# dK and dV of a sliding-window attention block made transposed on four column groups of TensorE, and W_up's late transposes issued earlier

## The chip, the cores and the metric

The kernel runs on one core of a Trainium2 chip. The metric is the device time of one execution in microseconds; a time is the median over several executions. A core has TensorE (PE in the profile, with its weight loads as PEld), VectorE (DVE), ScalarE (ACT), GpSimd (POOL) and SyncE (SP), each with its own instructions in order, and 16 DMA engines fed by queues that the engines issue to.

## What is computed

The kernel computes the output and all gradients of a gated mix of two branches: attention with a sliding window (32 heads of 16, window 256) and a feed-forward block with a ReLU gate. Cut to what matters:

```python
def _A_ref(x, wqkv, wo):
    B, S, D = x.shape                          # 1, 2048, 512
    H = 32; Dh = D // H; W = 256
    q, k, v = ...                              # (x @ wqkv), split into heads
    scores = jnp.einsum("bhqd,bhkd->bhqk", q, k) * (Dh ** -0.5)
    mask = (idx[:, None] - idx[None, :] >= 0) & (idx[:, None] - idx[None, :] < W)
    p = _softmax(jnp.where(mask[None, None], scores, -1e9), axis=-1)
    o = jnp.einsum("bhqk,bhkd->bhqd", p, v)
    return ... @ wo
def _B_ref(x, W_gate, W_up, W_down):           # F = 1376
    gate = x @ W_gate; up = x @ W_up
    return (gate * (gate > 0) * up) @ W_down

g = sigmoid((x * gate_w).sum(-1, keepdims=True))
out = g * _A_ref(x, A_wqkv, A_wo) + (1 - g) * _B_ref(x, B_W_gate, B_W_up, B_W_down)
# outputs: out and the gradients of x, wqkv, wo, W_gate, W_up, W_down, gate_w for a given grad_out
```

## The kernel before

Positions are cut into 16 tiles of 128 (NT), the 512 features into 4 column blocks (DC), each of which holds 8 heads (HG). There are three stages.

The first stage is the feed-forward block with its gradients in one loop over 11 blocks of F and 4 groups of 512 positions.

The second stage is the attention loop. Its order is written out by hand: an engine gets its instructions in the order in which the Python code emits them. The loop runs over turns (184 of them hold products). A turn takes two pairs of heads and up to two blocks of scores, each a query tile qb by a key tile kb, and emits in this order:

- `products`: on PE, the scores S of this turn and D = dO V^T of the turn before. Heads have 16 features, so these matmuls use 16 or 32 of the array's rows, and four row groups can work side by side.
- `front`: the exponential on ACT, from S in PSUM into PP in SBUF; `mask` on POOL; `gradp` on DVE, which multiplies PP by D.
- for some units, the transposed probabilities (`flip`): either a DMA transpose on SP's queue (line 779), or eight transposes on PE (line 787) into a PSUM tile `pt` and a copy out of it. The turned blocks lie in tiles P2, 14 buffers in all.
- `some_sums`: matmuls of `rowsum` (lines 746 and 748) with PP as weights, which collect row sums, the output and parts of dQ for a query tile in BA. When a query tile is complete ("closed"), BA is copied to BAs, and `small_ops` on DVE and POOL make from it `rq`, which holds, for each head, three groups of 16 columns: the first two are multiplied by P, the third by dS.
- `cd_piece`: two or more pieces a turn, three turns or more after the closing. A piece is four heads of one pair (kb, qb): for each head two matmuls (lines 497 and 500) with a turned block of P2 as 128 x 128 weights and 32 or 16 columns of rq streamed. They sum dK and dV of key tile kb in CD (one buffer), keys on the partitions. After a key tile's last piece, one copy brings CD to `rows_st`.
- PE flips, then `background` work: the next projections (`pp`), the transposes of K and V (`ptp`) and the gradient of wqkv of the column block before (`wps`).

The tiles `pt`, `ptp`, `pp` and `wps` share a tag "tr" of two PSUM buffers. CD and BA have one buffer each. `share` puts a copy on ACT or DVE, whichever has less work by a running estimate of costs (`busy`).

A list `plan` gives, by group of the projections, weight loads and DMA transposes of weights for the third stage; they wait in `late` and one of them is issued every second or fourth turn. The slots x0 to x3, d0 to d3 and p0 to p3, which hold inputs in transposed form at first, are used again for them.

The third stage goes over the 16 position tiles: `bps` (feed-forward output), `aps` (attention output), `dxps` (gradient of x, with W_gate, W_up and wqkv in turned form) and `wo_ps`. Its loads come by groups of two tiles (`load_group`). Between the second and the third stage stands a seam: the loads of group 0 (line 843 to 885), then the transposes of W_up for its blocks 4 to 10 (line 528), then `clear("Wu")`, which sets the rest of the last block to zero on POOL (line 531). In tile 0, the W_up part of dxps comes last.

Of the kernel before, what the change touches and what calls it, by code (L numbers as in the profile page):

```python
# [22 lines left out]
def kernel(  # L23
# [21 lines left out]
    P = 128  # L45
# [31 lines left out]

    busy = {"act": 0.0, "dve": 0.0}

    def share(out, in_, n, half=False, by=None, sbuf=False):  # L80
        cost = {"act": 0.11 + n * (0.00098 if sbuf else 0.00078),
                "dve": 0.08 + n * (0.00036 if sbuf else 0.00051 if half else 0.001)}
        eng = min(("act", "dve"), key=lambda e: busy[e] + cost[e])
        busy[eng] += cost[eng]
        if by is None:
            evac(out, in_, eng)
        elif eng == "act":
            nc.scalar.mul(out, in_, by)
        else:
            nc.vector.tensor_scalar(out, in_, by, None, op0=ALU.mult)  # L90
# [381 lines left out]
    if True:  # L472
# [8 lines left out]
        P2 = {}  # L481
        RQ = {}
        CDs = {}
        BAt = {}
        BAsb = {}
        sts = {}

        def cd_piece(c, kb, qb, half, last):
            if (c, kb) not in CDs:
                CDs[(c, kb)] = [psr.tile([P, HG, 2 * Dh], F32, tag="CD", bufs=1, name="CD"), True]  # L490
            cd = CDs[(c, kb)]
            rq = RQ[(c, qb)]
            for g in (2 * half, 2 * half + 1):
                p2 = P2[(c, qb, kb, g)]
                for pr in range(2):
                    h = 2 * g + pr
                    nc.tensor.matmul(cd[0][:, h, :], lhsT=p2[:, 0, pr, :], rhs=rq[:, h, 0:2 * Dh],  # L497
                                     start=cd[1], stop=True, skip_group_check=True)
                    cd[1] = False
                    nc.tensor.matmul(cd[0][:, h, 0:Dh], lhsT=p2[:, 1, pr, :], rhs=rq[:, h, 2 * Dh:3 * Dh],  # L500
                                     start=False, stop=True, skip_group_check=True)
            if last:
                share(sts[c][:, kb, 1:3, :].rearrange("p a (h d) -> p h a d", h=HG),
                      cd[0][:].rearrange("p h (a d) -> p h a d", a=2), 2 * P)
                if kb % 4 == 3 and (kb < NT // 2 or c == DC - 1):
                    spill(c, kb - 3)

        def spill(c, t0):
            tsl = slice(t0, t0 + NT // 4)
# [46 lines left out]
        def load_wo():  # L556
            for k0 in range(0, DC, 2):
# [6 lines left out]
                11: turns("wqkv", A_wqkv, 8, 12, "p2"),  # L564
                12: turns("Wg", B_W_gate, 0, 4, "x0") + turns("Wg", B_W_gate, 4, 8, "d0"),
                13: turns("Wg", B_W_gate, 8, 12, "x1") + turns("Wu", B_W_up, 0, 4, "d1") + [lambda: clear("Wg")],
                15: loads("Wd", B_W_down, 0, "x3") + loads("Wd", B_W_down, 4, "d3") + loads("Wd", B_W_down, 8, "p3") + [load_wo]}

        def grad_parts(c, seam=False):
            hold = {}  # L570
# [167 lines left out]
        def rowsum(u, i, qb, first, last):  # L738
            kb = u.blocks[i][1]
            kv = proj[(u.c, kb // TPG)]["kv"]  # L740
            if first:
                BAt[(u.c, qb)] = psr.tile([P, HG, 50], F32, tag="BA", bufs=1, name="BA")
            BA = BAt[(u.c, qb)]
            for pr in range(2):
                h = 2 * u.g + pr
                nc.tensor.matmul(BA[:, h, 0:33], lhsT=u.PP[:, 0, 2 * i + pr, :], rhs=kv[:, kb % TPG, h, 1:34],  # L746
                                 start=(first and pr == 0), stop=True, skip_group_check=True)
                nc.tensor.matmul(BA[:, h, 33:50], lhsT=u.PP[:, 1, 2 * i + pr, :], rhs=kv[:, kb % TPG, h, 0:17],  # L748
                                 start=False, stop=True, skip_group_check=True)
            if last:  # L750
                BAs = wk.tile([P, HG, 50], F32, tag="BAs", name="BAs")
                share(BAs[:], BA[:], HG * 50)
                BAsb[(u.c, qb)] = BAs

        def place(u):
            if u.edge:
                if u.at not in wides:
                    wides[u.at] = wide("p2")
                p2 = wides[u.at][:, u.x if u.nb == 2 else 0, :, :, :]
            elif u.at < 2 and u.x == 0:  # L760
                if "p2" not in wides:
                    wides["p2"] = wide("p2")
                p2 = wides["p2"][:, u.at, :, :, :]
            elif u.nb == 2 or u.x == 0:
                p2 = pools["p2"].tile([P, 2, 4, P], BF, tag="P2", bufs=14, name="p2")[:]
                wides[u.at] = p2
            else:
                p2 = wides[u.at]
            for i, (qb, kb) in enumerate(u.blocks):
                b = 2 * (i if u.nb == 2 else u.x)  # L770
                P2[(u.c, qb, kb, u.g)] = p2[:, :, b:b + 2, :]
            return p2
# [89 lines left out]
        def load_group(g):  # L862
# [15 lines left out]
                load_f(dgT_g, dgT_d, gsl)  # L878
            duT_g = S2["g6"].tile([P, FC, GT * P], BF, tag="duT_g")
            load_f(duT_g, duT_d, gsl)  # L880
            o_g = S2["g6"].tile([P, GT, DC, P], BF, tag="o_g", name="o_g")
            for t in range(GT):
                t0 = (g * GT + t) * P
                nc.sync.dma_start(o_g[:, t, :, :], dqkvo_d[t0:t0 + P, :].rearrange("p (c a n) -> p c a n", c=DC, a=4)[:, :, 3, :])
            nc.sync.dma_start(go_g[:] if g == 0 else go_g, go_d[gsl, :].rearrange("(t p) d -> p t d", p=P))
            return hT_g, dgT_g, duT_g, T_g, go_g, o_g

        with tc.manual_schedule():
# [47 lines left out]
                        break  # L936
                return total

            while turn < NI + 3 or ev or cdq or bg or sums:
                for e in busy:  # L940
                    busy[e] = max(0.0, busy[e] - 2.3) + (1.0 if e == "act" else 1.25)
                now = ev.pop(turn, [])
# [40 lines left out]
                if turn == 0:  # L983
                    behind.pop(0)()
                    behind.pop(0)()
                    background()
                    background()
                elif behind:
                    behind.pop(0)()
                if turn == 2:  # L990
                    fend.close()
                    pools["p2"] = p3b.enter_context(tc.tile_pool(name="attp2", bufs=2, side="right"))
# [2 lines left out]
                        flip(v)  # L995
                fresh = not sums or not sums[0][3] or (sums[0][0].c, sums[0][2]) == (0, 0) or turn > max(closed.values())
                some_sums(fresh)
                due = turn - 3 - closed.get(cdq[0][0:1] + cdq[0][2:3], turn) if cdq else 0
                for _ in range(4 if not us else 3 if due >= 3 else 2):
                    if cdq and closed.get(cdq[0][0:1] + cdq[0][2:3], turn) + 3 <= turn:  # L1000
                        piece = cdq.pop(0)
                        cd_piece(*piece)
                        if piece[4]:
                            break
                copies = []
                for w in flips.get(turn, []):
                    if not w.dma:
# [41 lines left out]
            S2["g6"] = ctx.enter_context(tc.tile_pool(name="g6", bufs=2))  # L1049
            S2["t6"] = ctx.enter_context(tc.tile_pool(name="t6", bufs=2))  # L1050
            grp_next = load_group(0)
            for f in turns("Wu", B_W_up, 4, 8, "x2") + turns("Wu", B_W_up, 8, 12, "d2"):
                f()
            clear("Wu")
            for f in S2["grads"]:
                store = f()
                if store is not None:
# [4 lines left out]
    with ExitStack() as p56:  # L1062
        x_r5 = x_r

        with ExitStack() as p6:
# [18 lines left out]
            for g in range(NG):  # L1084
# [3 lines left out]
                for tl in range(GT):  # L1088
# [27 lines left out]
                    amb = t6.tile([P, D], F32, tag="amb")  # L1116
                    nc.vector.tensor_tensor(out=amb[:], in0=a_sb[:], in1=bps[:], op=ALU.subtract)
                    nc.gpsimd.tensor_tensor(out=amb[:], in0=amb[:], in1=go_g[:, tl, :], op=ALU.mult)
                    dz = t6.tile([P, 4], F32, tag="dz")
                    nc.vector.reduce_sum(dz[:, 0:1], amb[:], axis=AX.X)  # L1120
                    nc.vector.tensor_tensor(out=dz[:, 1:2], in0=g_all[:, t:t + 1], in1=omg_all[:, t:t + 1],
# [89 lines left out]
```

## Time and profile before

| | us |
|---|---|
| median of 3 runs | 880.09 (880.01 to 880.79) |
| the profiled execution | 881.28 |
| its span from first to last instruction | 879.6 |
| PE busy in the span | 856.6 |
| DVE, POOL, ACT busy | 507.9, 478.5, 393.5 |
| mean granted clock of TensorE | 0.998 |

In the profile, a group of instructions has its line, engine, operation, the tiles written and read (buffer numbers left out), and its shapes; "128\*128 128x32" is a matmul with weights of 128 rows and 128 columns and a stream of 32. After the bar stand the busy time in us and the mean in ns of one, and after a second bar the engine's idle time just before the group with what ended it. Matmuls overlap in the array, so their durations add up to more than the time they take; the distance between starts tells their pitch. In a timeline the rows have start, duration, engine, line, operation, tiles and shapes, and neighbours of one kind are merged ("x8"). "SPq" is SP's issue of DMAs.

### The profile page before, as it was taken

Reading aid. Unit: us, or ns where it says so; the run is one execution under the profiler, and the core shown is the slowest. Engines: PE = TensorE matmul, PEld = TensorE weight load, DVE = VectorE, ACT = ScalarE, POOL = GpSimd, SP = SyncE. Lnnn points to the kernel's source line nnn. Section 1 sums busy time; section 2 is a strip of 40 time slices with the busy share of each in tenths; the row PEclk is TensorE's granted clock in tenths of the full one; section 3 lists DMA queues with packets and bytes.
Section 4 is the critical chain, followed back from the end, with each engine's and each line's share of the span. In section 5 each row is a group of like instructions: output and inputs, shape, how many; then the busy total and the mean of one; then the engine's idle time right before and its main releaser. Section 6 shows DMA issues by size and latency. Waiting matters only on the chain. (4 is left out here: it accounts for less than half of the span.)

```text
span 879.6 us, 29392 instructions
## 1 busy us (share of the span) xinstructions
PE 856.6 (97%) x12563; PEld 557.2 (63%) x12563; DVE 507.9 (58%) x764; ACT 393.5 (45%) x567; POOL 478.5 (54%) x887
## 2 busy tenths in 40 slices
PE   8999999999999999999999999999999899999998
PEld 5566655665567877767777777777777444444444
DVE  4445543333278888877888788887785132222223
ACT  5522222223366576756667666576654111111111
POOL 2644444444357777876778667786776222222111
PEclk9999999999999999999999999999999999999999
DMA  9999999999877999789998989999999999777731
GB/s 289 220 190 201 210 204 211 207 206 199 193 126 122 150 156 158 115 132 160 178 142 109 144 166 187 153 136 162 182 203 208 227 284 210 182 177 189 180 90 49
DMA packets 443132, 154.08 MB, mean 175 GB/s; under 512 B 371608, under 2 KB 440568, under 8 KB 443000
## 3 DMA queue, kind: packets, MB, share of 16 engines
q1 hardware_dynamic: 439400, 146.03, 88.7%
q0 software_dynamic: 2016, 5.64, 1.8%
q8 instruction: 98, 1.61, 0.8%
q10 hardware_dynamic: 1584, 0.53, 0.3%
q14 instruction: 34, 0.28, 0.1%
HBM read 32.15 MB, written 36.24 MB: 78 GB/s over the span
## 5 line engine op out<-in xcount | busy, mean ns | idle before, releaser
L729 DVE TENSOR_TENSOR PP<-PP,D 128x1024 bf16<-128x1024 bf16 (+1 forms) x184 | 219.0, 1190 | 53.8 <-POOL PP L722 17.5
L712 ACT ACTIVATE PP<-S 128x1024 bf16<-128x1024 f32 (+1 forms) x184 | 185.2, 1006 | 96.7 <-PE D L679 51.2
L722 POOL TENSOR_SCALAR_AFFINE_SELECT PP<-PP 128x512 bf16<-128x512 bf16 (+1 forms) x188 | 143.3, 763 | 77.7 <-ACT PP L712 75.3
L74 DVE COPY p<-pt 128x1024 bf16<-128x1024 bf16 x163 | 111.6, 685 | 10.6 <-PE pt L787 10.6
L356 POOL TENSOR_TENSOR hgu<-rg,upm 128x512 bf16<-128x512 bf16 x44 | 50.8, 1154 | 119.9 <-DVE upm L354 103.5
L787 PE MATMUL pt<-ident,PP 128*128 128x128 bf16 x1496 | 113.0, 218 | 0.1
L746 PE MATMUL BA<-KV,PP 128*128 128x33 bf16 x1440 | 106.6, 180 | 2.1 <-ACT BAs L72 1.6
L746 PEld LDWEIGHTS <-PP 128*128 128x128 bf16 x1440 | 85.7, 96 | 31.3 <-issue 11.7
L748 PE MATMUL BA<-KV,PP 128*128 128x17 bf16 x1440 | 102.4, 170 | 0.0
L396 PE MATMUL wps<-hgu_r,x_r 128*128 128x256 bf16 x640 | 96.0, 273 | 0.0
L497 PE MATMUL CD<-rq,p 128*128 128x32 bf16 x1440 | 94.8, 176 | 0.0
L500 PE MATMUL CD<-rq,p 128*128 128x16 bf16 x1440 | 93.6, 169 | 0.0
L748 PEld LDWEIGHTS <-PP 128*128 128x128 bf16 x1440 | 84.6, 96 | 10.9 <-issue 7.5
L787 PEld LDWEIGHTS <-PP 128*128 128x128 bf16 x1496 | 85.2, 97 | 0.2 <-issue 0.2
L497 PEld LDWEIGHTS <-p 128*128 128x128 bf16 x1440 | 80.7, 95 | 0.3
L500 PEld LDWEIGHTS <-p 128*128 128x128 bf16 x1440 | 80.5, 96 | 0.3
L396 PEld LDWEIGHTS <-x_r 128*128 128x128 bf16 x640 | 62.6, 98 | 28.3
L679 PE MATMUL S<-zT,K 32*128 32x128 bf16 (+3 forms) x1056 | 77.5, 238 | 0.4 <-ACT PP L712 0.2
L679 PE MATMUL D<-zT,V 32*128 32x128 bf16 (+3 forms) x1056 | 72.2, 237 | 4.9 <-DVE PP L729 4.3
L354 DVE SCALAR_TENSOR_TENSOR upm<-rg,ups 128x512 bf16<-128x512 bf16 x44 | 30.2, 687 | 80.3 <-PE ups L341 55.5
L1107 ACT COPY a_sb<-aps 128x512 f32<-128x512 f32 x16 | 9.3, 584 | 136.9 <-issue 107.3
L364 POOL TENSOR_TENSOR hgu<-dh_sb,rg 128x512 bf16<-128x512 bf16 x44 | 58.7, 1334 | 9.0 <-ACT dh_sb L362 9.0
(155 smaller groups left out, 1519.7 us busy)
## 6 DMA issues: line engine op xcount, KB each, us to landing
hgu_d<-hgu SPq DMA_DIRECT2D x44, 384.0 KB, 3.5
dqkvo_d<-rows_st SPq DMA_DIRECT2D x14, 512.0 KB, 4.5
duT_g<-hgu_d SPq DMA_DIRECT2D x8, 640.0 KB, 5.8
gt<-hgu_d SPq DMA_DIRECT2D x7, 640.0 KB, 5.9
dgT_g<-hgu_d SPq DMA_DIRECT2D x7, 640.0 KB, 4.9
p<-PP SPq DMA_TRANSPOSE x173, 4.0
out_dram<-wst SPq DMA_DIRECT2D x20, 128.0 KB, 3.0
go_in<-in_grad_out_dram SPq DMA_DIRECT2D x4, 512.0 KB, 8.7
```

The costliest lines, as they stand in the source:

```text
L74: nc.vector.tensor_copy(out, in_)
L364: nc.gpsimd.tensor_tensor(out=k.hgu[:, 2, :], in0=dh_sb[:], in1=k.rg[:], op=ALU.mult)
L396: nc.tensor.matmul(acc["w"][:, c, :], lhsT=x_r[:, t, c * P:(c + 1) * P], rhs=k.dgu_r[:, :, i, :], start=(go_ and c % 2 == 0), stop=no_, sk ...
L497: nc.tensor.matmul(cd[0][:, h, :], lhsT=p2[:, 0, pr, :], rhs=rq[:, h, 0:2 * Dh], start=cd[1], stop=True, skip_group_check=True)
L500: nc.tensor.matmul(cd[0][:, h, 0:Dh], lhsT=p2[:, 1, pr, :], rhs=rq[:, h, 2 * Dh:3 * Dh], start=False, stop=True, skip_group_check=True)
L679: nc.tensor.matmul(dst, lhsT=proj[(u.c, kb // TPG)][nm + ("", "1")[par]][rows[par], (kb % TPG) * P:(kb % TPG + 1) * P], rhs=proj[(u.c, qb ...
L712: nc.scalar.activation(two[:].rearrange("p x a b q -> p x a (b q)")[:, :, 0, 0:n], flat(us[0].S[:], n), ACT.Exp)
L722: nc.gpsimd.affine_select(out=out, in_=out, compare_op=ALU.is_ge, fill=0.0, base=0 if up else -1, pattern=[[0, 2], [0, b1 - b0], [1 if up ...
L729: nc.vector.tensor_tensor(out=v(1), in0=v(0), in1=flat(vs[0].D[:], n), op=ALU.mult)
L746: nc.tensor.matmul(BA[:, h, 0:33], lhsT=u.PP[:, 0, 2 * i + pr, :], rhs=kv[:, kb % TPG, h, 1:34], start=(first and pr == 0), stop=True, ski ...
L748: nc.tensor.matmul(BA[:, h, 33:50], lhsT=u.PP[:, 1, 2 * i + pr, :], rhs=kv[:, kb % TPG, h, 0:17], start=False, stop=True, skip_group_check ...
L787: nc.tensor.transpose(pt[:, a, b if u.nb == 2 else 2 * u.x + b, :], u.PP[:, a, b, :], ident[:])
```

## The change

In `cd_piece` the operands change places. The weights are now 32 or 16 columns of rq, and a turned block of P2 (128 columns) is streamed. The four heads of a piece write to four groups of 32 partitions of CD, so dK and dV are collected transposed, features on the partitions. `cd_piece` comes right behind the products in a turn, ahead of the sums. After a key tile's last piece, ACT copies CD to `cdT` in bf16; one turn later `cd_rows` (called from the list `backs`, ahead of the flips) turns it back by two transposes on PE into a "tr" buffer, `ptc`, and ACT copies that to `rows_st`. `share` gets an argument that names the engine; the copies of CD, ptc and BA name ACT. P2 has 13 buffers.

Of W_up's transposes, those of blocks 4 to 7 go into `plan`, behind the loads of W_down, and those of blocks 8 to 10 into `load_group(0)`, ahead of the loads of o and behind that of grad_out, which is itself ahead of the o loads now in each group. `clear("Wu")` is issued in tile 0 of the third stage, behind the product `amb` on POOL.

```diff
-    def share(out, in_, n, half=False, by=None, sbuf=False):
+    def share(out, in_, n, half=False, by=None, sbuf=False, eng=None):
...
-        eng = min(("act", "dve"), key=lambda e: busy[e] + cost[e])
+        eng = eng or min(("act", "dve"), key=lambda e: busy[e] + cost[e])
...
         def cd_piece(c, kb, qb, half, last):
             if (c, kb) not in CDs:
-                CDs[(c, kb)] = [psr.tile([P, HG, 2 * Dh], F32, tag="CD", bufs=1, name="CD"), True]
-            cd = CDs[(c, kb)]
+                CDs[(c, kb)] = psr.tile([P, 2, 2, P], F32, tag="CD", bufs=1, name="CD")
+            cd = CDs[(c, kb)][:, 0, :, :]
             rq = RQ[(c, qb)]
-            for g in (2 * half, 2 * half + 1):
-                p2 = P2[(c, qb, kb, g)]
-                for pr in range(2):
-                    h = 2 * g + pr
-                    nc.tensor.matmul(cd[0][:, h, :], lhsT=p2[:, 0, pr, :], rhs=rq[:, h, 0:2 * Dh],
-                                     start=cd[1], stop=True, skip_group_check=True)
-                    cd[1] = False
-                    nc.tensor.matmul(cd[0][:, h, 0:Dh], lhsT=p2[:, 1, pr, :], rhs=rq[:, h, 2 * Dh:3 * Dh],
-                                     start=False, stop=True, skip_group_check=True)
+            for a, d0, d1 in ((0, 0, 2 * Dh), (1, 2 * Dh, 3 * Dh)):
+                for h in range(4 * half, 4 * half + 4):
+                    r0 = 32 * (h % 4)
+                    nc.tensor.matmul(cd[r0:r0 + d1 - d0, half, :], lhsT=rq[:, h, d0:d1], rhs=P2[(c, qb, kb, h // 2)][:, a, h % 2, :],
+                                     start=(qb == kb and half == 0 and a == 0), stop=True, skip_group_check=True)
             if last:
-                share(sts[c][:, kb, 1:3, :].rearrange("p a (h d) -> p h a d", h=HG),
-                      cd[0][:].rearrange("p h (a d) -> p h a d", a=2), 2 * P)
-                if kb % 4 == 3 and (kb < NT // 2 or c == DC - 1):
-                    spill(c, kb - 3)
+                cdT = wk.tile([P, 2, P], BF, tag="cdT", name="cdT")
+                share(cdT[:], cd, 2 * P, eng="act")
+                backs.append((turn + 1, lambda: cd_rows(c, kb, cdT)))
+
+        def cd_rows(c, kb, cdT):
+            pt = ps.tile([P, 2, P], BF, tag="tr", bufs=2, name="ptc")[:]
+            for k in range(2):
+                nc.tensor.transpose(pt[:, k, :], cdT[:, k, :], ident[:])
+            share(sts[c][:, kb, 1:3, :].rearrange("p a (h d) -> p h a d", h=HG),
+                  pt.rearrange("p s (h a d) -> p (s h) a d", h=4, a=2), 2 * P, True, eng="act")
+            if kb % 4 == 3 and (kb < NT // 2 or c == DC - 1):
+                spill(c, kb - 3)
...
-                15: loads("Wd", B_W_down, 0, "x3") + loads("Wd", B_W_down, 4, "d3") + loads("Wd", B_W_down, 8, "p3") + [load_wo]}
+                15: loads("Wd", B_W_down, 0, "x3") + loads("Wd", B_W_down, 4, "d3") + loads("Wd", B_W_down, 8, "p3") + turns("Wu", B_W_up, 4, 8, "x2") + [load_wo]}
...
-                share(BAs[:], BA[:], HG * 50)
+                share(BAs[:], BA[:], HG * 50, eng="act")
...
-                p2 = pools["p2"].tile([P, 2, 4, P], BF, tag="P2", bufs=14, name="p2")[:]
+                p2 = pools["p2"].tile([P, 2, 4, P], BF, tag="P2", bufs=13, name="p2")[:]
...
             load_f(duT_g, duT_d, gsl)
+            nc.sync.dma_start(go_g[:] if g == 0 else go_g, go_d[gsl, :].rearrange("(t p) d -> p t d", p=P))
+            if g == 0:
+                for f in turns("Wu", B_W_up, 8, 12, "d2"):
+                    f()
             o_g = S2["g6"].tile([P, GT, DC, P], BF, tag="o_g", name="o_g")
...
-            nc.sync.dma_start(go_g[:] if g == 0 else go_g, go_d[gsl, :].rearrange("(t p) d -> p t d", p=P))
...
                 elif behind:
                     behind.pop(0)()
+                due = turn - 3 - closed.get(cdq[0][0:1] + cdq[0][2:3], turn) if cdq else 0
+                for _ in range(4 if not us else 3 if due >= 3 else 2):
+                    if cdq and closed.get(cdq[0][0:1] + cdq[0][2:3], turn) + 3 <= turn:
+                        piece = cdq.pop(0)
+                        cd_piece(*piece)
+                        if piece[4]:
+                            break
...
                 some_sums(fresh)
-                due = turn - 3 - closed.get(cdq[0][0:1] + cdq[0][2:3], turn) if cdq else 0
-                for _ in range(4 if not us else 3 if due >= 3 else 2):
-                    if cdq and closed.get(cdq[0][0:1] + cdq[0][2:3], turn) + 3 <= turn:
-                        piece = cdq.pop(0)
-                        cd_piece(*piece)
-                        if piece[4]:
-                            break
+                while backs and backs[0][0] <= turn:
+                    backs.pop(0)[1]()
...
             grp_next = load_group(0)
-            for f in turns("Wu", B_W_up, 4, 8, "x2") + turns("Wu", B_W_up, 8, 12, "d2"):
-                f()
-            clear("Wu")
...
                     nc.gpsimd.tensor_tensor(out=amb[:], in0=amb[:], in1=go_g[:, tl, :], op=ALU.mult)
+                    if t == 0:
+                        clear("Wu")
```

More of the change, by code (lines that the diff above doesn't have):

```diff
@@ L483 @@
         CDs = {}
+        backs = []
         BAt = {}
@@ L937, in some_sums @@
                 return total
-            while turn < NI + 3 or ev or cdq or bg or sums:
+            while turn < NI + 3 or ev or cdq or bg or sums or backs:
                 for e in busy:
```

## The prediction

> **What bounds the kernel now.** I read the page first, then the busy time by stretch, then the list of waits, then the timeline of some turns of the attention loop, and last the end of that loop.
>
> ```profile
> span 879.6 us, 29392 instructions
> ...
> PE 856.6 (97%) x12563; PEld 557.2 (63%) x12563; DVE 507.9 (58%) x764; ACT 393.5 (45%) x567; POOL 478.5 (54%) x887
> ```
> ```profile
> 400.00:500.00 100.00, 97.37 (x2305) 73.38 (x2303) 82.91 (x119) 66.23 (x92) 76.51 (x172) 1.00 0.99 143
> ...
> 670.00:710.00 40.00, 36.75 (x349) 20.68 (x346) 8.78 (x21) 7.52 (x15) 15.79 (x31) 0.96 1.07 246
> ```
> ```profile
> PE D L679 <- DVE PP L729: 4.3, 11, 0.6
> ```
>
> The columns of the stretches are length, then busy time (and instructions) of PE, PEld, DVE, ACT and POOL, the granted clock and the DMA share. The exponentials, one for each turn of the attention loop, span 240 to 668 us:
>
> ```profile
> L712 ACT ACTIVATE PP<-S x184: 592/1023/1044, 240.0 to 668.1; 128x1024 bf16<-128x1024 f32 x176, 128x512 bf16<-128x512 f32 x8
> ```
>
> In the middle of the loop PE is busy 97 of 100 us, while DVE has 17 us free and ACT 34. Among the waits (us in total, times, longest), PE's largest on another engine is 4.3 us in all. So PE's own order sets the time of the loop: what is taken from it shortens the loop, what is added or made to wait on it lengthens it. DMA is nearly full too (0.99), but no large wait of PE is for a turned tile of probabilities. A busy PE says nothing of its pitch, so the costs below are start-to-start distances in the timeline (start, duration, engine, line, operation, tiles, shapes, count).
>
> ```profile
> 453.52 0.28 PE L679 MATMUL S<-zT,K 16*128 16x256 bf16 x2
> 453.53 0.29 PE L679 MATMUL D<-zT,V 16*128 16x128 bf16 x4
> 453.64 0.27 PE L679 MATMUL S<-zT,K 32*128 32x256 bf16 x2
> 453.85 0.19 PE L746 MATMUL BA<-KV,PP 128*128 128x33 bf16 x1
> ...
> 454.27 0.18 PE L497 MATMUL CD<-rq,p 128*128 128x32 bf16 x1
> 454.29 0.17 PE L500 MATMUL CD<-rq,p 128*128 128x16 bf16 x1
> ...
> 454.85 0.17 PE L500 MATMUL CD<-rq,p 128*128 128x16 bf16 x1
> 454.87 0.61 PE L787 MATMUL pt<-ident,PP 128*128 128x128 bf16 x8
> 455.32 0.59 PE L149 MATMUL pp<-x,p 128*128 128x512 bf16 x2
> 455.84 0.28 PE L679 MATMUL S<-zT,K 16*128 16x256 bf16 x2
> 455.85 0.28 PE L679 MATMUL D<-zT,V 16*128 16x256 bf16 x2
> 455.96 0.27 PE L679 MATMUL S<-zT,K 32*128 32x256 bf16 x2
> 455.97 0.27 PE L679 MATMUL D<-zT,V 32*128 32x256 bf16 x2
> 456.17 0.19 PE L746 MATMUL BA<-KV,PP 128*128 128x33 bf16 x1
> ...
> 456.59 0.18 PE L497 MATMUL CD<-rq,p 128*128 128x32 bf16 x1
> ...
> 456.79 0.61 PE L787 MATMUL pt<-ident,PP 128*128 128x128 bf16 x8
> ```
> ```profile
> 453.96 1.02 ACT L712 ACTIVATE PP<-S 128x1024 bf16<-128x1024 f32 x1
> 456.28 1.02 ACT L712 ACTIVATE PP<-S 128x1024 bf16<-128x1024 f32 x1 [1.30 <-PE D L679]
> ```
> ```profile
> 717.91 4.75 PE dxps L1153 x22
> ```
>
> Five prices follow. (a) The 24 CD matmuls from 454.27 to 454.85 stand 0.58/23 = 25.2 ns apart, whether 32 or 16 columns wide. (b) 22 matmuls of 512 columns take 4.75 us, 216 ns each, 0.42 ns a column: 54 ns for 128 columns, 108 for 256. (c) Eight transposes start at 454.87 and the next matmul at 455.32: 0.45/8, 55 ns each. (d) In the products S and D four row groups run side by side: four matmuls of 256 columns start within 10 ns, the next four 120 ns later, that is 108 + 12; four of 128 columns would take 66. (e) Going over to row groups and back costs a gap: two wide matmuls from 455.32 end at 455.75 by (b) and S starts at 455.84, 0.09; the last D ends its stream at 456.08 and BA starts at 456.17, again 0.09.
>
> **What is removed.** 2,880 CD matmuls with 128-column weights (groups L497 and L500):
>
> ```profile
> L497 PE MATMUL CD<-rq,p 128*128 128x32 bf16 x1440 | 94.8, 176 | 0.0
> L500 PE MATMUL CD<-rq,p 128*128 128x16 bf16 x1440 | 93.6, 169 | 0.0
> ```
>
> At 25.2 ns that is 72.6 us of PE.
>
> **What replaces them.** As many matmuls, now with 32 or 16 weight columns and 128 streamed columns, in 720 sets of four, one for each column group. No row shows a column group. Lower bound: the four stream together without loss, 54 ns a set, 38.9 us. Upper bound: four weight loads one after another at the 25.2 of (a) and then an uncovered stream, 155 ns, 111.4 us. The nearest rows are the row groups of (d), where four streams and four loads interleave: 66 ns, 47.5 us. I take 47.5: a gain of 25.1 (between 33.7 and a loss of 38.8).
>
> **The drains.** CD now stands between products (row groups) and sums (full array). In the changed program's order of instructions, kinds of tiling change 552 times on PE instead of 370: 185 into products, 172 from products to CD, 177 from CD to full, 18 others. 182 more at 0.09 are 16.4 us. Lower bound: row to column groups costs nothing, since no row shows it; then 10 more are left, 0.9. The Trainium skill, TensorEngine Tiling (Array Packing), section Tiling Modes, says that a change of the tiling mode drains TensorE and does not except a change between two tilings; by it the 16.4 stand, by the lower bound the sum would be 15.5 us less.
>
> **The way back.** 64 keys' blocks by two transposes, 128 at 55 ns: 7.0 us, on PE's path, no cover.
>
> **The wait that is new.** The turned-back tile ptc takes one of the two "tr" buffers, which pt, pp, ptp and wps share. A background product holds one of them for much of the loop. In the changed program's order with its waits, in 26 of 64 cases the eight transposes pt right behind ptc wait for ACT's copy out of ptc, and in 32 cases the matmul behind those eight does; two more wait a turn later, two nowhere, two in the drain. PE is in order: all work of the turn behind it (transposes, background, the next products, so the next exponential) stands too. ACT is in order as well, and that copy comes behind the turn's exponential.
>
> ```profile
> L712 ACT ACTIVATE PP<-S 128x1024 bf16<-128x1024 f32 x176 | 180.4, 1025 | 94.4 <-PE D L679 51.2 <-PE S L679 33.1 <-ACT BAs L72 4.4
> ...
> L72 ACT CAST rows_st<-CD 128x256 bf16<-128x256 f32 x19 | 7.3, 382 | 7.7 <-PE CD L500 7.7
> ```
>
> The turn of 455.84, replayed: CD may start where BA did, 456.17; one piece of two sets 0.13, a drain 0.09, 16 sums from 456.17 to 456.59 before, 0.42: ptc at 456.81, free for more at 456.92. The exponential ends at 457.30, a copy of 0.38 at 457.68, and 0.04 of signal: wait 0.80. The turn of 453.52: its stream ends at 453.75, CD from 453.84, three pieces 0.40, drain 0.09, 16 sums 0.42, ptc 0.11, at 454.86; the exponential ends at 454.98, the copy at 455.40: 0.54. Mean 0.67; where eight transposes (0.44) lie between, 0.23. 26 x 0.67 + 32 x 0.23 = 24.8 us. Lower bound: ACT idle; then what is left of a transpose's 218 ns, 0.16, and the copy, 0.38, so 0.54 and 0.10, 17.2 us. Upper: 0.80 and 0.36, 32.3, and 0.49 for a BAs copy behind the exponential in 9 cases: 36.7.
>
> ```profile
> L787 PE MATMUL pt<-ident,PP 128*128 128x128 bf16 x1496 | 113.0, 218 | 0.1
> ...
> L72 ACT COPY BAs<-BA 128x400 f32<-128x400 f32 x64 | 31.5, 492 | 0.0
> ```
>
> **Moved between engines.** ACT gets 128 copies of 0.38 and loses 19, while 12 copies of pt go to DVE and 10 of KV come: by the counts of the changed program +35 us for ACT, -16 for DVE. ACT goes from 66 to about 74 of 100: hidden by PE, if the BAs copies don't get late for the next sums. Bounds 0 and half a cdT copy in 64 turns, 12; I take 3, as ACT keeps a quarter free. P2 with 13 buffers for 14: CD now reads earlier in its turn, and turned tiles are asked for some four turns (of 2.3 us, 453.52 to 455.84) after their issue, against 4.0 from issue to landing:
>
> ```profile
> p<-PP SPq DMA_TRANSPOSE x173, 4.0
> ```
>
> So nothing, and one turn (2.3) for each tile that would be late.
>
> **W_up's transposes.** The seam now:
>
> ```profile
> 688.33 3.35 SPq L528
> 691.72 1.46 SPq L528
> ...
> 694.57 4.65 DMA d<-in_B_W_up_dram
> ```
> ```profile
> 698.31 0.59 PE L1153 MATMUL dxps<-d,duT_g 128*128 128x512 bf16 x2 [1.94 <-DMA d<-in_B_W_up_dram]
> 699.83 0.58 PE L1153 MATMUL dxps<-d,duT_g 128*128 128x512 bf16 x1 [0.93 <-POOL d L531]
> 700.21 1.91 PE L1094 MATMUL bps<-x,f 128*128 128x512 bf16 x4
> 701.92 1.69 PE L1094 MATMUL bps<-d,f 128*128 128x512 bf16 x4
> 703.45 0.81 PE L1094 MATMUL bps<-p,f 128*128 128x512 bf16 x3
> ```
>
> PE idles 1.94 and 0.93, and afterwards eight matmuls take 3.24 instead of 8 x 0.216 = 1.73 (clock 0.96 in this stretch): 1.5. Together 4.4. Two transposes (688.33 to 693.18 on SP's queue) now go out in the loop's last turns, ahead of the four loads "early", where nothing waits for them; the loads behind them on SP are later by those 4.85 us at most, and their data are asked for after the loop. The other two go ahead of the o loads, so d lands at least 4.85 sooner, by 694.4 instead of 699.2, and PE asks for it at 698.31 - 1.94 = 696.4. The clearing goes behind amb on POOL, which go_g's earlier load brings forward as well. What remains is the drain of the loop: the last CD goes through ACT, PE and ACT again, 0.5 late at most, as products wps stand beside it. I take -4 (bounds -4.4 and +0.5).
>
> **The sum.** -25.1 + 16.4 + 7.0 + 24.8 + 3 - 4 = +22.1. The profiled execution took 881.28 (span 879.6 and 1.7 around it), so 903.4; the median of the runs shown, 880.09, lies 1.2 below, so 902.
>
> **The rivals.**
>
> Faster: column groups without stagger or drain. Sets at 54 ns (-33.7), row to column free (+0.9), transposes +7.0, waits at their least (+17.2), ACT nothing, seam -4.4: -13.0, 867. For it: four streams start within 10 ns in the products. Against it: the 12 ns above the stream and both gaps there. With the waits left at 24.8 both must hold nearly whole before it decides: 22.1 - 8.6 (sets at 54) - 15.5 (no such gap) = -2.0.
>
> Slower still: narrow weight loads do not overlap each other. At 25.2 ns each with the stream hidden, CD costs 72.6 as before: 902 + 25 = 927; with the stream bare 966. For it: CD's pitch now doesn't depend on its columns, so a load or an issue sets it. Against: in the products four matmuls with a load each start within 10 ns. The Trainium skill, TensorE: Matmul & The Clock Gate, section LDWEIGHTS (loading the stationary operand), puts a load at its columns over 1.2 GHz, and the Trainium skill, TensorEngine Tiling (Array Packing), section Restrictions and Gotchas, says that column tiling has no fast weight load; as an estimate by these, 4 x 27 + 4 x 13 = 160 ns a piece, 57.6 us, and the sum would be 912. No run here shows it.
>
> The seam doesn't gain: the clearing on POOL, behind amb, ends after PE asks for it, and the clock falls as now: 906.
>
> **How the numbers follow.** Forecast 0.56 with a range of its own from 888 to 918 (waits 17 to 37, drains 1 to 16); faster rival 0.21; slower still 0.15; no gain at the seam 0.05; 0.03 for an end within 0.2% (some 1.8 us, about what a measurement of this kernel can tell from no change). The range reaches to the faster rival and to 927 with its own spread: 866 to 932. Faster 0.21, same 0.03, slower 0.76.
>
> **What would show it.** CD starts in sets of four with 66 ns between sets; 0.09 between the last product and CD and between CD and BA; the list of waits with pt and pp behind ACT's copy of rows_st at some 25 us, now absent; DVE's and ACT's busy time as counted; no PE wait on W_up, and clock 1.00 behind the seam. Wrong if PE doesn't wait on those copies, or if sets stand 100 ns apart.

## The result, and the profile after

| | before | after |
|---|---|---|
| median, same chip, us | 880.44 (880.01 to 881.28) | 908.26 (907.79 to 908.68) |
| ratio | | 1.0312 [1.0293, 1.0331] |
| span of the profiled execution, us | 879.6 | 906.8 |

The change costs 27.8 us; 22.1 were forecast (902 forecast, 908.3 measured). The head of the page of the changed kernel, with its exponentials:

```profile
span 906.8 us, 29638 instructions
...
PE 848.2 (94%) x12569; PEld 532.3 (59%) x12691; DVE 501.7 (55%) x721; ACT 422.0 (47%) x674; POOL 481.3 (53%) x887
```
```profile
L717 ACT ACTIVATE PP<-S x184: 591/1024/1042, 240.1 to 697.3; 128x1024 bf16<-128x1024 f32 x176, 128x512 bf16<-128x512 f32 x8
```

The head has to be read with care: it counts 12569 matmuls (PE) for 12691 weight loads (PEld), where before the two are equal. The records of 122 matmuls are missing from this trace, 72 of them of the projections `pp` in the loop, at 0.216 us each. So PE's busy time is up to 26 us too low here and can't be set against the 856.6 of before, and a wait behind a missing matmul looks longer than it was. Starts, spans and medians don't suffer from this.

The span rose by 27.2. The attention loop, read by its exponentials, lasts 457.2 instead of 428.1. By the trace's starts, from the loop's first product to its last, it is 459.8 instead of 430.3: 29.5 longer. The stretch from there to the third position tile of the third stage is 2.3 shorter. So the loop is the whole loss. Two stretches of the changed kernel (columns as before: length, busy time of PE, PEld, DVE, ACT, POOL, clock, DMA share, GB/s):

```profile
400.00:500.00 100.00, 89.90 (x2153) 63.43 (x2165) 75.05 (x99) 66.84 (x106) 71.14 (x158) 1.00 0.86 138
500.00:600.00 100.00, 90.77 (x2145) 63.46 (x2160) 74.41 (x99) 64.92 (x103) 70.11 (x155) 1.00 0.94 148
```

PE idles 10.1 of the first 100 us by the row, where it idled 2.6. Twelve matmuls are missing there (2153 for 2165 weight loads), some 2.6 us, so 7.5 is nearer. No other engine is near full, the DMA share is lower than the 0.99 of before, and the clock is whole: this is waiting, not a new engine that bounds. What PE waits for, in the list of waits (us in total, times, longest):

```profile
PE pt L792 <- ACT rows_st L72: 14.6, 26, 0.9
PE BA L751 <- ACT BAs L72: 14.1, 33, 0.6
PE D L684 <- DVE PP L734: 4.6, 13, 0.6
PE pp L149 <- DVE p L74: 2.5, 7, 0.4
PE pp L149 <- ACT rows_st L72: 2.3, 6, 0.5
PE dxps L1162 <- DMA d<-in_B_W_up_dram: 2.1, 1, 2.1
```

The first line is the forecast wait: 26 times, as counted. The second is one that I had nearly left out; before, that line stood at 1.6 us:

```profile
PE BA L746 <- ACT BAs L72: 1.6, 6, 0.3
```

Of the 14.1, some 3 us are missing matmuls: 17 of the 33 waits stand behind `pp`, each with one matmul on record for two weight loads. Two kernels below that have a copy out of CD in the same place, and whose traces are complete, list 11.4 and 11.1; I go by about 11. PE's timeline shows a turn, the next one's sums, and a case of each wait:

```profile
456.46 0.41 PE L497 MATMUL CD<-p,rq 128*32 128x128 bf16 x16
456.80 0.19 PE L751 MATMUL BA<-KV,PP 128*128 128x33 bf16 x1
...
457.45 0.39 PE L187 MATMUL ptp<-ident,V 128*128 128x128 bf16 x4
458.44 0.18 PE L751 MATMUL BA<-KV,PP 128*128 128x33 bf16 x1 [0.60 <-ACT BAs L72]
...
458.85 0.27 PE L684 MATMUL D<-zT,V 32*128 32x256 bf16 x2
459.05 0.52 PE L497 MATMUL CD<-p,rq 128*32 128x128 bf16 x24
459.50 0.19 PE L751 MATMUL BA<-KV,PP 128*128 128x33 bf16 x1
...
462.38 0.29 PE L497 MATMUL CD<-p,rq 128*32 128x128 bf16 x8
462.60 0.19 PE L751 MATMUL BA<-KV,PP 128*128 128x33 bf16 x1
...
480.60 0.27 PE L507 MATMUL ptc<-ident,cdT 128*128 128x128 bf16 x2
481.76 0.44 PE L792 MATMUL pt<-ident,PP 128*128 128x128 bf16 x5 [0.89 <-ACT rows_st L72]
```

The runs of 8, 16 and 24 CD matmuls start 0.22, 0.34 and 0.45 ahead of BA: each two sets of four cost 0.11 to 0.12. Over all such runs the starts give 59 ns a set on average (56 in two cases of three, 67 in most others), and 3 to 4 ns between matmuls of a set. From D to CD it is 0.20, of which 0.108 is D's own stream: a gap of 0.09, as between row groups and the full array. From the last CD to BA it is 0.152, of which 0.054 is CD's stream: again a gap of 0.1. ACT in the same turn:

```profile
456.70 1.03 ACT L717 ACTIVATE PP<-S 128x1024 bf16<-128x1024 f32 x1
457.62 0.38 ACT L72 CAST cdT<-CD 128x256 bf16<-128x256 f32 x1
457.87 0.52 ACT L72 COPY BAs<-BA 128x400 f32<-128x400 f32 x1
```

Here is the second wait: cdT's copy stands between the exponential and the copy of BA. BA has one buffer, so the sums at 458.44 wait until BAs is done. ACT's starts put the price of cdT's copy at 0.25 (457.62 to 457.87), as the copies overlap a little. In the changed program 51 of the 64 BAs copies stand right behind a cdT copy.

The seam, in the timelines of SP, POOL and PE:

```profile
714.76 0.43 SPq L886 DMA_DIRECT2D go_g<-in_grad_out_dram  x1
715.24 6.35 SPq L533 DMA_TRANSPOSE d<-in_B_W_up_dram  x2
```
```profile
728.60 0.52 POOL L536 MEMSET d<- 32x512 bf16 x1 [10.05 <-DMA d<-in_B_W_up_dram]
...
729.63 1.17 POOL L1125 TENSOR_TENSOR amb<-amb,go_g 128x512 f32<-128x512 f32 x1
```
```profile
728.29 0.59 PE L1162 MATMUL dxps<-d,duT_g 128*128 128x512 bf16 x2 [2.08 <-DMA d<-in_B_W_up_dram]
729.16 0.38 PE L1162 MATMUL dxps<-d,duT_g 128*128 128x512 bf16 x1 [0.28 <-POOL d L536]
729.38 1.02 PE L1101 MATMUL bps<-x,f 128*128 128x512 bf16 x3
```

PE still waits 2.08 us for W_up, though two of its transposes went out in the loop. But the matmuls behind it run at full speed (bps at 216 ns), and the clock is 1.00 where it was 0.96. POOL's rows show one thing more: the clearing (the MEMSET) is written behind `amb` in the code, but it stands ahead of it on POOL. Outside the attention loop, the order on an engine is thus not always the order of the code.

### The profile page after: what moved, and what is told of

It reads as the page before. It is cut to its first block, busy times and chain, and to the rows that moved or that the text cites. A ratio compares the mean times of both kernels' runs of the same rounds, so it can differ in the third digit from the quotient of the medians.

```text
span 906.8 us, 29638 instructions
## 1 busy us (share of the span) xinstructions
PE 848.2 (94%) x12569; PEld 532.3 (59%) x12691; DVE 501.7 (55%) x721; ACT 422.0 (47%) x674; POOL 481.3 (53%) x887
## 5 line engine op out<-in xcount | busy, mean ns | idle before, releaser
L74 DVE COPY p<-pt 128x1024 bf16<-128x1024 bf16 x175 | 120.1, 687 | 30.0 <-PE pt L792 29.6
L792 PE MATMUL pt<-ident,PP 128*128 128x128 bf16 x1496 | 113.2, 218 | 14.6 <-ACT rows_st L72 14.6
L751 PE MATMUL BA<-KV,PP 128*128 128x33 bf16 x1440 | 106.5, 180 | 14.3 <-ACT BAs L72 14.1
L751 PEld LDWEIGHTS <-PP 128*128 128x128 bf16 x1440 | 85.6, 96 | 26.1 <-issue 0.4
L792 PEld LDWEIGHTS <-PP 128*128 128x128 bf16 x1496 | 88.1, 97 | 17.9 <-issue 17.7
L753 PEld LDWEIGHTS <-PP 128*128 128x128 bf16 x1440 | 84.5, 96 | 22.5 <-issue 19.8
L684 PE MATMUL S<-zT,K 32*128 32x128 bf16 (+3 forms) x1056 | 75.6, 238 | 2.8 <-ACT PP L717 0.2
L497 PE MATMUL CD<-p,rq 128*16 128x128 bf16 (+1 forms) x2880 | 72.7, 222 | 0.0
L347 ACT ACTIVATE rg<-gps 128x512 bf16<-128x512 f32 x44 | 26.3, 597 | 81.8 <-PE gps L341 81.0
L497 PEld LDWEIGHTS <-rq 128*16 128x16 bf16 (+1 forms) x2880 | 40.5, 92 | 25.9 <-issue 11.8
L398 PE MATMUL dps<-db_r,hgu_r 128*128 128x512 bf16 x145 | 55.0, 379 | 0.0
```

The source lines that it names most:

```text
L74: nc.vector.tensor_copy(out, in_)
L497: nc.tensor.matmul(cd[r0:r0 + d1 - d0, half, :], lhsT=rq[:, h, d0:d1], rhs=P2[(c, qb, kb, h // 2)][:, a, h % 2, :], start=(qb == kb and ha ...
L684: nc.tensor.matmul(dst, lhsT=proj[(u.c, kb // TPG)][nm + ("", "1")[par]][rows[par], (kb % TPG) * P:(kb % TPG + 1) * P], rhs=proj[(u.c, qb ...
L792: nc.tensor.transpose(pt[:, a, b if u.nb == 2 else 2 * u.x + b, :], u.PP[:, a, b, :], ident[:])
```

## The experiments

Times are medians in us on one chip beside the kernel before, ratios are against that kernel with a 95% interval, and "the loop" is the distance from its first product to its last.

**The way back taken out.** From the changed kernel:

```diff
             if last:
-                cdT = wk.tile([P, 2, P], BF, tag="cdT", name="cdT")
-                share(cdT[:], cd, 2 * P, eng="act")
-                backs.append((turn + 1, lambda: cd_rows(c, kb, cdT)))
+                share(sts[c][:, kb, 1:3, :], cd, 2 * P, eng="act")
...
```

> The changed kernel without the way back: no cdT, no transposes ptc; ACT copies CD straight to rows_st (so the rows of dK and dV stay transposed within a key tile: the turning back is left out). Theory (the way back costs the time: 7 us of transposes and some 31 us of PE waiting, directly or behind the flips, for ACT's copy out of ptc): about 908 - 38 = 870, no wait of pt on rows_st left, the wait of BA on BAs still about 14. Rival (the column groups' drains and the new place of the pieces cost it, the way back little): about 908 - 7 = 901, PE idle elsewhere instead.

876.66 (875.99 to 878.63), ratio 0.996 [0.9946, 0.9973]; loop 428.4. This kernel leaves out the turning back, so its dK and dV stay transposed within a key tile; it tells a cost and is no candidate. The way back costs 908.26 - 876.66 = 31.6 (38 were expected); without it the time is some 4 us below before. Its list of waits has no wait of pt for `rows_st`, but still:

```profile
PE BA L751 <- ACT BAs L72: 11.4, 31, 0.6
```

One ACT copy out of CD is left ahead of BAs, so this wait belongs to where that copy stands, not to the turning back.

**The sums first, then CD.** The block with `cd_piece` goes behind `some_sums`, ahead of the way back:

```diff
-                due = ...
-                for _ in range(4 if not us else 3 if due >= 3 else 2):
-                    ...
...
                 some_sums(fresh)
+                due = ...
+                for _ in range(4 if not us else 3 if due >= 3 else 2):
+                    ...
```

> The changed kernel with CD's pieces behind the first sums again, where they stood before. Theory: products to sums to CD to full array makes 172 more changes of tiling at about 0.095 us (+16), and the 0.3 us of CD stand again between a closing sum and the next opening one, so that the wait of BA on BAs falls from 14 to about 2 (-12): about 912. Rival (a drain costs only when it comes from the products, and the new place is what lost the time): 896.

909.19 (908.86 to 911.55), ratio 1.0331 [1.0317, 1.0345]; loop 460.7.

```profile
PE pt L792 <- ACT rows_st L72: 14.0, 26, 0.8
PE BA L751 <- ACT BAs L72: 1.4, 6, 0.2
```

BAs is copied ahead of cdT now and its wait is down to 1.4 from about 11; yet the loop is 0.9 longer. What this order adds is 172 more changes between tilings (products to sums to CD to transposes). By the starts, a step from the sums to CD takes 100 ns, where the step from the sums to the transposes took 25: 0.075 x 172 = 12.9. The fall of the wait pays back some 10 of it; 2 to 3 us more that came back are not assigned. So the place of `cd_piece` was a fair exchange. The time alone doesn't tell the two costs apart; the starts and the list of waits do.

**Only cdT's copy later.** The copy goes to a list and is issued behind `some_sums`; PE's order stays:

```diff
             if last:
-                cdT = ...
+                def out_of_cd():
+                    cdT = wk.tile([P, 2, P], BF, tag="cdT", name="cdT")
+                    share(cdT[:], cd, 2 * P, eng="act")
+                    backs.append((turn + 1, lambda: cd_rows(c, kb, cdT)))
+                outs.append(out_of_cd)
...
                 some_sums(fresh)
+                while outs:
+                    outs.pop(0)()
```

> The changed kernel with ACT's copy of CD to cdT issued behind the first sums, so behind the copy of BA in ACT's queue and not ahead of it (in the changed kernel 51 of 64 BAs copies stand right behind a cdT copy). Theory (BA waits because the 0.38 us copy of CD stands ahead of BAs): the wait of BA on BAs falls from 14 to below 4, about 908 - 10 = 898. Rival (BAs is late because of the exponential ahead of both): unchanged, 906 to 908.

900.05 (899.32 to 901.21), ratio 1.0219 [1.0203, 1.0234]; loop 451.4, 8.4 less.

```profile
PE BA L755 <- ACT BAs L72: 2.8, 10, 0.3
PE pt L796 <- ACT rows_st L72: 14.6, 26, 0.9
```

The order of two copies on ACT alone is worth 8.2 us. That is what the wait for BAs fell by, from about 11 to 2.8; this trace has all its matmuls (12691). The other wait is untouched.

**ptc out of the shared buffers.** The two turning matmuls write to the unused half of the next key tile's CD buffer (58 of 64 times; else to "tr"):

```diff
         def cd_rows(c, kb, cdT):
-            pt = ps.tile([P, 2, P], BF, tag="tr", bufs=2, name="ptc")[:]
-            for k in range(2):
-                nc.tensor.transpose(pt[:, k, :], cdT[:, k, :], ident[:])
+            nxt = (c, kb + 1) if kb + 1 < NT else (c + 1, 0)
+            if nxt in CDs and live[0] == nxt:
+                pt = CDs[nxt][:, 1, :, :]
+                for k in range(2):
+                    nc.tensor.matmul(pt[:, k, :], lhsT=cdT[:, k, :], rhs=ident[:], start=False, stop=True, skip_group_check=True)
+            else:
+                ...
```

> The changed kernel with the turned-back tile ptc not in a tr buffer but in the free half of the next key tile's CD buffer (a matmul with the identity; 58 of 64 cases, the others stay in tr). All copies on ACT and all transposes on PE stay. Theory (PE loses about 25 us by waiting for a tr buffer): no wait of pt or pp on rows_st, some of it comes back as wait of BA on BAs, which ACT serves no earlier: 908 - 25 + 5 = 888. Rival (ACT's added load sets the pace, whichever buffer is waited for): above 900, BA's wait grown by about as much as pt's fell.

885.22 (884.23 to 885.92), ratio 1.0044 [1.0029, 1.0059]; loop 435.5, 24.3 less. The wait of pt for ACT's copy out of ptc has left the list, and of pp's 2.3 us 0.9 are left; of the BAs wait there remains:

```profile
PE BA L760 <- ACT BAs L72: 11.1, 30, 0.6
```

That is 3.0 less than the changed kernel's list says, but its trace lacks that much in matmuls of `pp`: behind every tile other than `pp`, the waits for BAs in the two traces agree within 0.01 us. So this wait did not change, and the "tr" buffer alone cost 24.3. ACT still makes the same copies, so its load as such is not the cause. The transposes themselves are still there.

**Both repairs**, the last two edits together:

> Both repairs: ptc in the CD buffer and the copy of CD behind BAs in ACT's queue. Theory: 900.1 - 25 = 875, with at most 5 us of waits of PE on ACT; that is the column groups at their own price: streams -32, changes of tiling +17, transposes +7, so 872 and some waits. Rival (ACT's load): above 890.

877.9 (876.65 to 880.36), ratio 0.9967 [0.9954, 0.998]: faster than both kernels, by 2.5 and 30 us. Loop 428.9.

```profile
PE D L698 <- DVE PP L748: 3.7, 10, 0.6
PE BA L765 <- ACT BAs L72: 2.8, 10, 0.3
```

PE's largest wait is once more the one of before, for DVE's product.

**Both repairs with W_up's old order**: the same kernel with `load_group`, `plan` and `clear("Wu")` as before the change:

```diff
-... + turns("Wu", B_W_up, 4, 8, "x2") + [load_wo]}
+... + [load_wo]}
...
             grp_next = load_group(0)
+            for f in turns("Wu", B_W_up, 4, 8, "x2") + turns("Wu", B_W_up, 8, 12, "d2"):
+                f()
+            clear("Wu")
```

> Both repairs of e6, with W_up's transposes, the clearing and the go loads where the kernel before has them. The loop of e6 took 428.9 us from the first to the last product, against 430.3 before. Theory (in e6 the gain at the seam, not the loop, makes the rest): the loop's -1.4 stays, the seam is as before: 879 to 880. Rival (the W_up part gives nothing here either, as in e4): as e6, 878.

879.29 (876.62 to 881.55), ratio 0.9982 [0.9971, 0.9994]; loop 429.0, equal. So W_up's new place is worth 879.29 - 877.9 = 1.4, and the intervals of the two ratios overlap.

**W_up alone**, on the kernel before (the W_up edits of the change, nothing else):

> The kernel before with the change's W_up part alone (transposes earlier, go loads ahead of the o loads, clearing behind amb). As read from the seam of the changed kernel (PE still waits 2.1 us for the second W_up tile, but the clock stays up): 880.4 - 2.5 = 877.9. The prediction's figure: -4, 876.4. Rival (a wash): 880.

880.12 (878.21 to 882.45), ratio 0.9988 [0.9975, 1.0001]: at most 0.25% of gain, and none is not excluded. In the timelines of SP and ACT of before, grad_out's load and its first use:

```profile
686.69 1.59 SPq L885 DMA_DIRECT2D go_g<-in_grad_out_dram  x1
```
```profile
693.41 1.33 ACT L1111 ACTIVATE da_b<-go_g,g_all 128x512 bf16<-128x512 bf16 x2 [6.88 <-DMA go_g<-in_grad_out_dram]
```

With the W_up edits alone, the timelines of SP, ACT and PE show what took the place of the wait:

```profile
690.40 0.43 SPq L881 DMA_DIRECT2D go_g<-in_grad_out_dram  x1
```
```profile
695.73 1.33 ACT L1111 ACTIVATE da_b<-go_g,g_all 128x512 bf16<-128x512 bf16 x2 [8.36 <-DMA go_g<-in_grad_out_dram]
```
```profile
685.82 0.39 PE L1094 MATMUL bps<-x,f 128*128 128x512 bf16 x1 [0.92 <-DMA f<-hgu_d]
...
697.81 0.38 PE L1155 MATMUL dxps<-d,duT_g 128*128 128x512 bf16 x1 [0.16 <-POOL d L531]
699.55 1.02 PE L1094 MATMUL bps<-x,f 128*128 128x512 bf16 x4 [1.37 <-DVE amb L1117]
```

PE no longer waits for the transposes. But they stand in SP's queue ahead of the loads of group 0, and all of these are later. `f` comes 0.92 late for the first bps. go_g goes out at 690.40 instead of 686.69, although it now stands ahead of the o loads, so ACT's da_b starts at 695.73 instead of 693.41, `ga` comes behind it, then `amb`, which has to read bps's buffer before the next tile's bps may write it: 1.37. In sum PE waits 2.45, where it waited 1.94 + 0.93 = 2.87.

**The seam in another order.** All four transposes ahead of the o loads, go_g on POOL's queue, `clear` behind `amb`: first on the kernel before, then with both repairs.

```diff
+            (nc.gpsimd if g == 0 else nc.sync).dma_start(go_g...)
+            if g == 0:
+                for f in turns("Wu", B_W_up, 4, 8, "x2") + turns("Wu", B_W_up, 8, 12, "d2"):
+                    f()
             o_g = ...
```

> The kernel before with all four W_up transposes in the seam, ahead of the o loads, the load of grad_out on POOL's queue, and the clearing behind amb; nothing is added ahead of the loads early and f on SP's queue. Theory (the W_up part gained nothing because its two transposes delay SP's queue in the loop's last turns, so that f and grad_out land later): PE waits for neither d, f nor amb for more than 0.5 us, 880.6 - 4 = 876.6. Rival (the seam is limited by what the DMA engines can move): 880.

880.66 (878.12 to 884.25), ratio 1.0 [0.9984, 1.0017].

```profile
685.05 7.14 SPq L528 DMA_TRANSPOSE x<-in_B_W_up_dram  x2
692.24 7.17 SPq L528 DMA_TRANSPOSE d<-in_B_W_up_dram  x2
```
```profile
698.48 0.59 PE L1155 MATMUL dxps<-x,duT_g 128*128 128x512 bf16 x2 [1.61 <-DMA x<-in_B_W_up_dram]
```

They start 3.3 us earlier than before, and take 14.3 us in SP's queue instead of 7.45: PE waits for x, which it did not do, 1.61. The earlier issue gained nothing, against the 4 us expected.

> Both repairs of e6 with the seam of e7. Theory: e6 - 3.5, about 872, under both kernels. Rival: as e6 or above the kernel before.

882.58 (880.13 to 883.58), ratio 1.0018 [1.0008, 1.0029]: 10 us above the 872 expected; this seam takes back what the repairs gave. The longest wait in its seam:

```profile
PE dxps L1178 <- DMA x<-in_B_W_up_dram: 2.9, 2, 1.9
```

**All of W_up within the loop.** All four transposes in `plan`: on the kernel before, with both repairs, and with both repairs and `clear("Wu")` written behind `amb`.

```diff
-... + [load_wo]}
+... + turns("Wu", B_W_up, 4, 8, "x2") + turns("Wu", B_W_up, 8, 12, "d2") + [lambda: clear("Wu"), load_wo]}
```

> The kernel before with all four W_up transposes and the clearing in the plan of the loop, behind the loads of W_down, none in the seam (the rest as in the change's W_up part). Theory (the seam is full of transfers, and what is taken from it and put into the loop shortens it, against later loads early and f): no wait of PE on d; waits on f and amb of 1 to 2 us as in e4; 880.4 - 2 = 878.5. Rival (each transfer ahead of early gives back what it takes away): 880 to 881.

> Both repairs of e6 with the W_up part of e9. Theory: e6 less what the second tile's wait costs there, 877. Rival: 878 to 880, no better than e6.

> e10 with the clearing behind amb in tile 0, so that POOL doesn't wait for the second tile's transposes ahead of rq. Theory (the 8.1 us wait of CD on POOL's rq was the clearing waiting for the DMA): that wait is gone, 884.5 - 7 = 877. Rival (the transposes in SP's queue delay early and f as well): 880 or more, with PE waiting for f.

886.46, 884.5 and 887.65; ratios 1.0065 [1.0051, 1.0079], 1.0044 [1.0029, 1.006] and 1.0077 [1.0064, 1.009]. All three are slower, against the 877 to 878.5 expected, by one long wait of PE for POOL: 7.3, 8.1 and 10.2 us. The third kernel, in its list of waits and in POOL's timeline:

```profile
PE CD L500 <- POOL rq L831: 10.2, 1, 10.2
```
```profile
668.75 0.40 POOL L840 TENSOR_TENSOR rows_st<-t,rinv 128x128 bf16<-128x128 f32 x1
681.11 0.51 POOL L550 MEMSET d<- 32x512 bf16 x1 [11.95 <-DMA d<-in_B_W_up_dram]
681.59 0.19 POOL L825 TENSOR_TENSOR ndel<-BAs,rinv 128x8 f32<-128x8 f32 x1
681.75 0.39 POOL L826 TENSOR_TENSOR rq<-rows,rinv 128x128 bf16<-128x128 bf16 x1
```

The clearing needs the last transpose to have landed. It stands on POOL ahead of the small operations that make rq for the last query tiles, and these stand behind it for 11.95 us. The third kernel was to show the loop without this, and it didn't: although written behind `amb`, the clearing stands on POOL six operations earlier than in the second, ahead of rq for two query tiles instead of one. So the cause of the wait is shown by the row, but what all four transposes in the loop would be worth without it was not measured.

## Why the prediction was right, and where not

The direction, the mechanism and the size hold: 908.3 against 902 with 888 to 918 as the forecast's own range. By terms:

- **CD's streams and the drains** (forecast -25.1 + 16.4 = -8.7): -10.9 by the distances from CD to CD and from CD to what follows. Sets stand 59 ns apart on average, not 66, nearer to the lower bound of 54. The gap between products and CD is 0.09, so going from row to column groups is not free. The Trainium skill, TensorEngine Tiling (Array Packing), section Tiling Modes, whose drain at every change of mode was weighed there, is borne out by these 0.09. The slower rival (loads that don't overlap) needed 100 ns a set and falls. The estimate of 160 ns for a piece of two sets, from the Trainium skill, TensorE: Matmul & The Clock Gate, section LDWEIGHTS (loading the stationary operand), is not borne out either: a piece takes 117 on average.
- **The faster rival** had its sets almost, but neither the free change of tiling nor the short waits nor the seam. Its point of decision was that sets and change hold nearly whole; one did.
- **The way back and its wait** (7.0 + 24.8 = 31.8): the loop without it is 459.8 - 428.4 = 31.4 shorter. Taking ptc out of "tr" alone gave 24.3, which leaves 7.1 for the transposes. By the starts in the changed kernel, 26 transposes pt stand 0.72 later behind ptc than the 55 ns of a transpose, and in 32 cases the matmul behind the eight does, by 0.25. So both counts were right, and the means (0.67 and 0.23) nearly. The sign that was named, some 25 us in the list of waits, did not come that way: the list has 14.6 + 2.3, as it counts from the modelled end of a transpose of 218 ns and leaves out what is shorter.
- **"ACT keeps a quarter free"** (3, bounds 0 and 12): this is the step that failed in size. The BAs wait went from 1.6 to about 11.1, +9.5, three times what I took and inside the bounds. I judged by ACT's share of busy time, and had the bound right at hand: half a cdT copy in each turn with a closing. The copy is ahead of BAs in 51 of 64 cases, and PE comes to the next sums just then. ACT is indeed a third idle (66.84 of 100 busy), which did not help.
- **W_up "ahead of 'early', where nothing waits for them"** (-4): failed. From the loop's end to the third tile 2.3 us were gained in the profiled executions; by the medians, alone on the kernel before between nothing and 2.2 by the ratio's interval, beside the repairs 1.4. I did count the 4.85 us by which the loads behind are later, and said that their data are asked for after the loop; they are, but f and go_g were asked for then with less than 4.85 to spare. In the changed kernel's trace the transposes of d take 6.35 us of SP's queue instead of 2.60, and d is late again; without the way back, with cdT's copy later and with both repairs, the seam is the same and PE has no such wait. "The clearing goes behind amb" did not come about either: it stands ahead of `amb` on POOL, 728.60 and 729.63.
- **ACT's and DVE's share**: ACT +28.5 us (forecast +35), DVE -6 (forecast -16). Neither bounds.
- **P2 with 13 buffers, 0**: holds; no wait of PE on a turned tile is in the list.

Worked out from the loop: -10.9 + 31.4 + 9.5 = 30.0 against 29.5 measured; -0.5 is not assigned. The forecast's +22.1 was short by 6.5 for BAs and 1.7 for W_up (2.6 by the repairs' 1.4), and long by 0.4 for the way back and 2.2 for CD. So the total is a little nearer than its terms: errors of 2.6 one way hid a part of some 8 the other way.

## What to carry to other kernels

A cheaper stream on a full TensorE is worth what its results then cost: here 11 us were gained by the streams and lost three times over (24.3 + 9.5) to one shared PSUM buffer and one copy's place, which two small edits won back. For each copy that a change adds, look up behind and ahead of which copies it stands on its engine and how many buffers their tiles have; a share of idle time says nothing of that. Before a DMA is moved earlier on a queue, list what stands behind it there with the slack of each, the loads of the next stage too. Where an instruction stands on its engine is read from the trace, not from the code. And before two traces are compared by busy time or waits, compare their counts of matmuls and weight loads: here missing records made one wait 3 us too long.

## What the runs showed of the hardware

Weight loads of 16 and 32 columns cost at most 5 ns a set when they go to four column groups in turn: four loads and four streams of 128 columns take 59 ns on average, against 54 for the stream alone. Two pairs of DMA transposes from DRAM took 7.14 and 7.17 us in SP's queue where they had taken 4.85 and 2.60 when issued 3.3 us later; the DMA share of the 40 us from 670 is 1.06 and 1.07, so the mean doesn't tell why. And the granted clock of the 40 us from 670 fell in some of the kernels in which PE idled in the seam, but not by the length of the idle time alone. It was 0.96 where waits of 1.94 and 0.93 came close together (before), and 0.96 too with 0.35, 0.94 and 0.44 close together (W_up's old order beside the repairs). It was 1.00 in the W_up-alone kernel, whose waits of 0.92 and 1.37 lie some 14 us apart, and 1.00 in the changed kernel's 40 us from 700, with 2.08 and 0.28. With one wait of 7.3, 8.1 and 10.2 (all of W_up in the loop) it was 0.87, 0.91 and 0.83; the last row:

```profile
670.00:710.00 40.00, 29.61 (x290) 15.98 (x289) 4.55 (x9) 7.91 (x17) 12.41 (x27) 0.83 0.79 190
```

Part of what a wait in the seam costs can thus be paid after it, in slower matmuls (before: eight in 3.24 us instead of 1.73). From which idle time that begins, these traces don't show.
